# Regrouping TensorE's half-array products and postponing VectorE work in a fused mLSTM and Fourier-mixing kernel

## The chip, the cores and the metric

One core of one Trainium2 chip. The metric is the device time of one execution in microseconds; the profile's span is some 1.7 us shorter (421.29 and 419.6 for the kernel before). Every execution told of here was of the fast state. A ratio is the mean time of one kernel's fast runs over that of the kernel before in the same rounds, so it is not quite the ratio of the medians quoted beside it.

## The reference, cut to what matters

```python
# mLSTM cell: batch 4, 8 heads, 768 tokens, head size 40
for t in range(S):
    m_new = np.maximum(f_gate[:, :, t] + m, i_gate[:, :, t])
    ...
    C = f_stab * C + i_stab * np.einsum('bhd,bhe->bhde', vt, kt)
    n = f_stab * n + i_stab * kt
    y[:, :, t] = o * (C @ qt) / np.maximum(np.abs(n @ qt), 1.0)
# Fourier mixing, normalisation and an MLP of 320 -> 1280 -> 320
mixed = np.real(np.fft.fft(np.fft.fft(x, axis=1), axis=2))
u = x + mixed
un = (u - mu) / np.sqrt(var + 1e-06)
out = u + np.maximum(un @ w_ch1, 0.0) @ w_ch2
```

The kernel takes the recurrence in six chunks of 128 tokens per batch. While the MLP of batch b runs, the chunks of batch b+1 run beside it. Everything is placed by hand in slots, so that TensorE always has a product to do.

## The kernel before: the parts concerned

`at(slot, phase, ...)` enters work in a plan; the program is emitted in the order (slot, phase). The phases are EVAC 0, FILL 1, MAIN 2, FILL_PE 3. Engines run their own share of that order and wait for each other by semaphores.

```python
EVAC, FILL, MAIN, FILL_PE = range(4)
ps_s = pool("ps_s", 2, space=PSUM)
ps_h = pool("ps_h", 2, space=PSUM)     # ph, pc and (most) px take these two in turn
...
def mlstm_from_state(b, c):            # 128 rows: the full array (L479)
    k.ph = ps_h.tile([L, NP, L], FP, name="ph", tag="ph")
    ... nc.tensor.matmul(k.ph[:, p, :], k.C[:, p, :], k.qg[:, p, :], start=(p == 0), stop=False)
...
# in plan_mlstm(b, s0); chunk c is at s = s0 + 3 * c
at(s, FILL_PE + 2, mlstm_scores, b, c)              # 40 rows (L465)
at(s + 2, FILL, mlstm_weigh, b, c)                  # VectorE (L471)
at(s + 3, FILL_PE, mlstm_from_state, b, c)
at(s + 3, FILL_PE + 3, mlstm_from_chunk, b, c)      # L486
at(s + 3, FILL_PE + 3, mlstm_to_state, b, c)        # L496, into pc
t = s + (8, 8, 7, 5, 5, 5)[c]                       # batches after the first
at(t, FILL_PE + 1, mlstm_turn, b, c)                # transpose into px (L535)
at(t + 1, FILL + 0.05, mlstm_finish, b, c)          # VectorE reads px (L544 to L550)
...
def mlp_in(b, gr, f):                               # MLP of batch 0: 320 = 128 + 64 + 128 features
    if f % 2 == 0:
        k.pm = [bank("pm", [L, TG * L]) for _ in range(2)]
    for i, ch in ((1, 1),) if f % 2 else ((0, 0), (0, 1), (1, 0)):
        nc.tensor.matmul(k.pm[i], w1_sb[:, ch, f0:f0 + L], u[2 * ch], start=(ch == 0), stop=False)   # L837
    if f % 2:
        for i in range(2):                          # 64 rows each, side by side in the array (L841)
            r = slice(i * TAIL, (i + 1) * TAIL)
            nc.tensor.matmul(k.pm[i], w1t_sb[r, f // 2 * L:(f // 2 + 1) * L], u[1][r], start=False, stop=True)
...
# MLP of batches 1 to 3, one block in four slots (cut): L897 products, then the tails (L902, 64 rows)
add(h12, p5)                     # step 1, VectorE (L906): the first add
tails(1, (p3, p5)); tails(0, (p2, p1))
add(h12, p3); add(h22, p5); add(h11, p2)            # step 2: the other three
```

L479 and the like are lines of the kernel. A pair of 64-row products uses the two halves of the array at once: in the records the second starts 6 to 7 ns after the first. "Excursion" below means TensorE leaving the full array for such products and coming back. A PSUM bank holds what TensorE has summed until another engine has read it; only then can the next product that is given the bank start.

VectorE's other work has short names below. The finish of a chunk divides and writes its output. The conversions (L344 to L364, in part on ScalarE) prepare weights that have come in by DMA. The fold prepares the Fourier mixing's input, rstd is the reciprocal of the standard deviation (its steps alternate between VectorE and GpSimd), and the weight sum adds blocks of weights. GpSimd also makes each chunk's mask (L443) and scales its queries (L431).

## Time and profile before

| | before |
|---|---|
| median of the first 3 executions | 422.48 us (421.55 to 423.32) |
| span of the profile | 419.6 us |
| TensorE busy | 407.0 us, 97% |
| VectorE busy | 288.5 us, 69% |
| TensorE's idle gaps of over 30 ns, summed from the records | 9.5 us |

TensorE is the bound. Its idle time is small, so a reader should distrust the word "busy": the steps between its matmuls show where a busy TensorE runs slower than it can. The lines for this, and the waits, are in the prediction.

### The profile page before, as it was taken

The numbers are of one execution on the slowest core, as the hardware profiler recorded it, in microseconds if no ns is written. First come the engines' busy times: TensorE is split into PE (matmuls) and PEld (weight loads), VectorE is DVE, ScalarE is ACT, GpSimd is POOL, SyncE is SP. The second block draws the span as 40 slices with busy tenths as digits, with TensorE's granted clock in tenths as the row PEclk, the third lists the DMA queues.
The fourth block names the chain that finished last, engine by engine and source line by source line (L and its number), as shares of the span: only waits on it lengthen the run. The fifth ranks groups of instructions, "written<-read, shape, count | busy, mean of one in ns | idle before, by whom it ended". The sixth has DMA issues, their size and how long they took to land.

```text
span 419.6 us, 8013 instructions
## 1 busy us (share of the span) xinstructions
PE 407.0 (97%) x2966; PEld 304.0 (72%) x2966; DVE 288.5 (69%) x682; ACT 189.1 (45%) x493; POOL 112.9 (27%) x194
## 2 busy tenths in 40 slices
PE   8999999999999999999899999999999999999997
PEld 6877455566567778777458998977559988555996
DVE  8789895777995638795955578795854686335652
ACT  6986376586561222654356413654452023355000
POOL 5554201468331520342131440342120000020000
DMA  7899297557665144266200344310000000000010
GB/s 240 285 252 301 86 284 242 195 178 222 215 182 164 58 155 136 67 210 172 75 0 2 136 151 135 107 46 2 0 2 0 33 31 22 12 2 0 16 48 31
DMA packets 20549, 47.14 MB, mean 112 GB/s; under 512 B 2784, under 2 KB 9312, under 8 KB 20384
## 3 DMA queue, kind: packets, MB, share of 16 engines
q1 hardware_dynamic: 20512, 46.65, 35.8%
q8 instruction: 23, 0.38, 0.4%
q14 instruction: 14, 0.11, 0.1%
HBM read 42.52 MB, written 4.11 MB: 111 GB/s over the span
## 4 chain that ended last, share of the span: by engine, by line
PE 81%; DVE 12%; ACT 2%; issue 2%; DMA 1%; POOL 0%; DVEq 0%; ACTq 0%; POOLq 0%
PE po L1016 19%; PE pm L897 15%; PE po L960 8%; PE pm L837 5%; PE ps L465 5%; PE ph L486 5%; PE pm L902 4%; PE ph L479 4%; PE pu L729 4%; PE put L772 2%; PE px L535 2%; PE pz L698 2%; PE pm L841 1%; DMA raw<-in_w 1%; PE pz L686 1%
## 5 line engine op out<-in xcount | busy, mean ns | idle before, releaser
L966 DVE SCALAR_TENSOR_TENSOR x<-po,rstd,x 128x160 f32<-128x160 f32 (+1 forms) x69 | 27.0, 394 | 41.4 <-PE po L1016 35.5
L906 DVE TENSOR_TENSOR h<-h,pm 128x384 f32<-128x384 f32 x60 | 30.5, 549 | 31.4 <-PE pm L897 16.0
L421 ACT ACTIVATE W<-W,colT 128x128 f32<-128x128 f32 x144 | 45.0, 396 | 0.0
L443 POOL TENSOR_SCALAR_AFFINE_SELECT W<-W 128x1024 f32<-128x1024 f32 x18 | 21.3, 1183 | 79.8 <-ACT W L421 58.7
L897 PE MATMUL pm<-uT,w_sb 128*128 128x384 f32 x90 | 37.5, 503 | 1.8 <-DVE h L906 1.6
L960 PE MATMUL po<-w_sb,h 128*128 128x320 f32 x120 | 34.4, 435 | 0.0
L471 DVE TENSOR_TENSOR W<-ps,W 128x512 f32<-128x512 f32 x48 | 30.7, 680 | 4.5 <-POOL W L443 4.3
L837 PE MATMUL pm<-uT,w_sb 128*128 128x384 f32 x80 | 29.6, 499 | 0.7 <-DVE x L749 0.5
L777 ACT COPY uT<-put 128x384 f32<-128x384 f32 x24 | 11.2, 478 | 40.2 <-PE put L772 40.2
L960 PEld LDWEIGHTS po<-w_sb,h 128*128 128x128 f32 x120 | 22.2, 190 | 9.5 <-issue 0.8
L1016 PE MATMUL po<-T,S 128*128 128x160 f32 x180 | 27.9, 302 | 0.3 <-DVE x L966 0.3
L465 PE MATMUL ps<-qk 40*128 40x128 f32 x384 | 27.8, 284 | 0.0
L792 POOL TENSOR_TENSOR t<-rstd 128x6 f32<-128x6 f32 x12 | 3.1, 261 | 88.5 <-DVE v L790 87.9
L1016 PEld LDWEIGHTS po<-T,S 128*128 128x128 f32 x180 | 25.5, 190 | 1.7 <-DVE x L966 0.5
L897 PEld LDWEIGHTS pm<-uT,w_sb 128*128 128x128 f32 x90 | 15.5, 189 | 15.4 <-DVE h L906 7.7
L1016 PE MATMUL po<-w_sb,h 128*128 128x160 f32 x180 | 26.4, 301 | 0.0
L465 PEld LDWEIGHTS ps<-qk 40*128 40x128 f32 x384 | 23.4, 187 | 4.1 <-issue 0.7
L1016 PEld LDWEIGHTS po<-w_sb,h 128*128 128x128 f32 x180 | 25.1, 190 | 1.3 <-DVE x L966 0.3
L486 PE MATMUL ph<-W,kvt 128*41 128x128 f32 x384 | 25.8, 277 | 0.0
L524 ACT COPY h<-ph 41x512 f32<-41x512 f32 (+1 forms) x16 | 9.3, 583 | 36.2 <-PE ph L486 36.0
L431 POOL TENSOR_TENSOR qg<-qk,Gb 128x512 f32<-128x512 f32 x18 | 25.0, 1390 | 0.1
L479 PEld LDWEIGHTS ph<-qg,C 128*128 128x128 f32 x160 | 19.9, 191 | 6.8 <-issue 3.3
(207 smaller groups left out, 865.6 us busy)
## 6 DMA issues: line engine op xcount, KB each, us to landing
W<-M_d SPq DMA_DIRECT2D x18, 512.0 KB
kvt<-in_kv SPq DMA_DIRECT2D x24, 324.0 KB
qk<-in_qkT SPq DMA_DIRECT2D x48, 160.0 KB
raw<-in_w SPq DMA_DIRECT2D x10, 640.0 KB
Gb<-G_d SPq DMA_DIRECT2D x36, 128.0 KB
so<-in_o SPq DMA_DIRECT2D x24, 160.0 KB
out<-x SPq DMA_DIRECT2D x24, 160.0 KB
ds_sb<-in_dft_s SPq DMA_DIRECT2D x1, 1155.0 KB
```

Of the source, the lines that this page charges most:

```text
L421: nc.scalar.activation(out=k.W[:, h, :], in_=M, func=AF.Exp, scale=-1.0, bias=colT[:, c, 0, b * H + h:b * H + h + 1])
L431: nc.gpsimd.tensor_tensor(out=k.qg, in0=k.qk[:, 0], in1=k.Gb, op=OP.mult)
L465: nc.tensor.matmul(k.ps[hip][:, p, :], k.qk[r, 1, p, :], k.qk[r, 0, p, :], start=True, stop=True)
L471: nc.vector.tensor_tensor(out=Wv, in0=k.ps[hip], in1=Wv, op=OP.mult)
L479: nc.tensor.matmul(k.ph[:, p, :], k.C[:, p, :], k.qg[:, p, :], start=(p == 0), stop=False, skip_group_check=True)
L486: nc.tensor.matmul(k.ph[hip * 64:hip * 64 + D1, p, :], k.v1[:, 2 * p + hip, :], k.W[:, 2 * p + hip, :], start=(c == 0 and p == 0), stop=Tr ...
L837: nc.tensor.matmul(k.pm[i], w1_sb[:, ch, f0:f0 + L], u[2 * ch], start=(ch == 0), stop=False)
L897: nc.tensor.matmul(bank, w, u, start=start, stop=True, skip_group_check=True)
L906: nc.vector.tensor_tensor(out=h, in0=h, in1=bank, op=OP.add)
L960: nc.tensor.matmul(k.po, hidden(gr, f)[:, i * L:(i + 1) * L], w2_sb[:, f, :], start=(f == 0), stop=(f == NFF - 1))
L966: nc.vector.scalar_tensor_tensor(out=u, in0=po, scalar=k.rstd[:, c:c + 1], in1=u, op0=OP.mult, op1=OP.add)
L1016: nc.tensor.matmul(po, a[:, f], w[:, f], start=start and f == 0, stop=f == half - 1, skip_group_check=True)
```

## The change

Its intent is to make TensorE change between the full array and half-array products less often, and to take VectorE's less urgent work out of the way of the adds that free PSUM banks.

```diff
+    slots_of_halves = (32, 38, 50, 65, 97)
...
-            at(s + 2 if end else s + 3, FILL_PE, mlstm_from_state, b, c)
+            at(s + 2 if end else s + 3, MAIN - 0.1 if s + 3 in slots_of_halves else FILL_PE, mlstm_from_state, b, c)
...
-                t = s + (8, 8, 7, 5, 5, 5)[c]
+                t = s + (8, 8, 7, 7 if b == 1 else 5, 5, 5)[c]
...
-            at(x_done[j], FILL + 0.5 if b < 2 else FILL_PE + 0.2, mix_fold, b, p)
+            at(x_done[j] + (b > 1 and j == TG - 1), FILL + 0.5 if b < 2 else FILL_PE + 0.2, mix_fold, b, p)
...
+        ahead = gr == 1 and f // 2 in (1, 3)
         if f % 2 == 0:
-            k.pm = [bank("pm", [L, TG * L]) for _ in range(2)]
+            k.pm = k.pm_next if ahead else [bank("pm", [L, TG * L]) for _ in range(2)]
...
+        if f % 2 and not ahead:
+            between(k.pm, f // 2, False)           # the 64-feature products of this pair
+            if gr == 1 and f // 2 < NFF // 2 - 1:  # and those of the next pair, which start its banks
+                k.pm_next = [bank("pm", [L, TG * L]) for _ in range(2)]
+                between(k.pm_next, f // 2 + 1, True)
...
-        done = [s_mlstm + 3 * (j + NT // 2) + 7 for j in range(NT // 2)]
+        done = [s_mlstm + 3 * (j + NT // 2) + 7 + (b == 1 and j == 0) for j in range(NT // 2)]
...
-        at(s_mlp + NFF, FILL + 0.6, mix_rstd, b)
+        at(s_mlp + NFF + (2 if b > 0 else 0), FILL + 0.6, mix_rstd, b)
...
-        at((56, 57, 58, 72)[n], FILL + 0.4, out_weight_sums, n)
+        at((56, 57, 58, 75)[n], FILL + 0.4, out_weight_sums, n)
```

More of the change, by code (lines that the diff above doesn't have):

```diff
@@ L832, in mlp_in, with between @@
         u = [uT_bufs[gr][:, ch].rearrange("p c t -> p (c t)") for ch in range(3)]
+        def between(pm, n, start):
+            for i in range(2):
+                r = slice(i * TAIL, (i + 1) * TAIL)
+                nc.tensor.matmul(pm[i], w1t_sb[r, n * L:(n + 1) * L], u[1][r], start=start, stop=not start,
+                                 skip_group_check=True)
+        ahead = gr == 1 and f // 2 in (1, 3)
         if f % 2 == 0:
-            k.pm = [bank("pm", [L, TG * L]) for _ in range(2)]
+            k.pm = k.pm_next if ahead else [bank("pm", [L, TG * L]) for _ in range(2)]
         for i, ch in ((1, 1),) if f % 2 else ((0, 0), (0, 1), (1, 0)):
             f0 = (f // 2 * 2 + i) * L
-            nc.tensor.matmul(k.pm[i], w1_sb[:, ch, f0:f0 + L], u[2 * ch], start=(ch == 0), stop=False)
-        if f % 2:
-            for i in range(2):
-                r = slice(i * TAIL, (i + 1) * TAIL)
-                nc.tensor.matmul(k.pm[i], w1t_sb[r, f // 2 * L:(f // 2 + 1) * L], u[1][r], start=False, stop=True)
+            nc.tensor.matmul(k.pm[i], w1_sb[:, ch, f0:f0 + L], u[2 * ch], start=(ch == 0 and not ahead),
+                             stop=(ch == 1 and ahead), skip_group_check=True)
+        if f % 2 and not ahead:
[3 more added lines that the diff above has]
+                between(k.pm_next, f // 2 + 1, True)
     hid = {}
```

## The prediction

> **What bounds the kernel now.** I read the page's busy row first, then the chain that ended last, then who TensorE waited for, then the chain in order of time around each place that the diff touches.
>
> ```profile
> span 419.6 us, 8013 instructions
> PE 407.0 (97%) x2966; PEld 304.0 (72%) x2966; DVE 288.5 (69%) x682; ACT 189.1 (45%) x493; POOL 112.9 (27%) x194
> PE 81%; DVE 12%; ACT 2%; issue 2%; DMA 1%; POOL 0%; DVEq 0%; ACTq 0%; POOLq 0%
> PE pm L897 <- DVE h L906: 1.6, 2, 1.1
> PE ph L479 <- DVE den L544: 0.9, 1, 0.9
> ```
>
> TensorE is busy 97% and carries 81% of the chain, so only two things can shorten the program: less time inside TensorE's own stream, or fewer of its waits. The list of TensorE's waits is short. Summed over its gaps it idles about 9.5 us, and half of that lies before 60 us, where nothing changes. The last two lines above are the waits that the change can reach: 1.6 us in two stops of the MLP blocks (1.06 us at 207.94, 0.55 us at 301.97), and 0.9 us before one group of partial products from the state (L479) at 110.23.
>
> A busy TensorE hides a second cost. These are pieces of the chain in order of time (start, us until the next piece, what):
>
> ```profile
> 79.29 0.84 PE pm L841 x4
> 80.14 1.09 PE ph L479 x8
> 81.22 1.09 PE ps L465 x16
> ...
> 88.12 1.94 PE pm L837 x6
> 90.06 0.89 PE ph L479 x8
> 90.95 1.09 PE ps L465 x16
> ...
> 113.76 0.84 PE pm L837 x2
> 114.61 0.84 PE pm L841 x4
> 115.45 2.13 PE pm L837 x6
> ```
>
> L837 and L479 contract over 128 rows; L841 is the pair of 64-feature products, one on each half of the rows, and L465 works on 40 rows. After L837 the eight passes of L479 take 0.89 us; after L841 the same eight take 1.09. Six passes of L837 take 1.94 us in steady state and 2.13 after L841. So coming back to the full array costs 0.20 us. Going in costs as much: in the records the first L841 starts 416 ns after the last L837 where 322 is the steady step, and the next step is 420 where two products side by side repeat at 316. Going in and out is thus 0.20 + 0.20 = 0.40 us. From L841 straight into L465 (both on part of the rows) the records show no such step.
>
> **What the Trainium skill says.** The page "TensorEngine Tiling (Array Packing)", section "Key Properties", says that changing the tiling mode, and not merely the tile, drains TensorE, and that different tiles work in parallel. The trace agrees: about 0.1 us extra on each of two steps at every change of mode, and the second product of a pair starts 6 to 7 ns after the first. "SBUF — State Buffer", section "Who interferes with whom", says that only the port pair shared by VectorE and GpSimd contends, as an exclusive lock. The trace agrees where the weight conversion L358 takes 0.82 us at 91.28 and 1.64 at 111.64, beside GpSimd's mask (L443); this decides how soon VectorE is done below. "Perfetto Trace Analysis", section "Tensor Engine Instruction (MATMUL, LD_WEIGHTS)", says that TensorE's end times are computed, not observed; hence I use start-to-start steps.
>
> **The change, part by part.** The instructions are the same; ACT's and SP's order is unchanged, and only TensorE, VectorE and GpSimd are reordered.
>
> (1) The products from the state go ahead of the last MLP products of their slot. Of the five slots named, 32 holds none (batch 1 has 35, 38, ... 50), so four groups move: slots 38 and 50 in batch 1 (80.14 and 119.51 above), 65 in batch 2 (187.66) and 97 in batch 3 (282.49). Each stood between 64-row and 40-row products and so cost a way out and in again: 4 x 0.39 = 1.57 us gross.
>
> (2) The 64-feature products of two pairs stand together twice: two fewer excursions, 2 x 0.39 = 0.79 us gross. Starting a bank with them instead of with the 128-row product adds no instruction. The banks are free early enough: their ReLUs run at 88.67 and 99.13, and the banks are wanted after 94 and 105.
>
> (3) In batch 1 the turn of chunk 3 moves two slots back. Then L479 at 110.23 no longer needs the bank of the turn that VectorE finishes only at 110.09, and 0.91 us of wait goes. But the last L479 (slot 50) now needs the bank of this late turn. I follow VectorE: it ends the finish of chunk 2 near 109.7, then converts weights (2.5 to 3.5 us), adds the state (0.67), weighs (1.29) and finishes chunk 3 (1.65), which gives 116 to 117; TensorE arrives near 116.3. So nothing to 0.7 us comes back.
>
> (4) One place keeps TensorE from using what it gains: L479 of slot 44 waits for the query scaling on GpSimd (0.08 us now, at 99.18). GpSimd is full with 12 steps of rstd from 91.4 to 96.7, and only the 0.39 us of slot 38 moves it forward. TensorE would arrive about 0.8 us earlier and wait about 0.45.
>
> Sum for the first MLP (57.9 to 123): 4 x 0.39 (slots 38 and 50, and (2)) + 0.91 - 0.04 (an exit that was cheaper into the turn) - 0.4 - 0.3 = about 1.7 us.
>
> (5) Slots 65 and 97 gain a wait. The moved L479 (of batch 2 and 3, beside the MLP of the batch ahead) takes the bank of the turn of chunk 2, and in the built program it now waits for VectorE, which before it did not. In batch 2 VectorE ends that finish at 185.11 (L550 from 184.62 for 0.49 us), while TensorE would be there at 184.7: 0.5 us of wait against 0.39 saved, net -0.1. In batch 3 two subtractions are slowed by GpSimd (1.32 and 1.51 us instead of 0.56), so the finish ends at 280.42 and TensorE would be there at 279.2: L479 from 280.5, its 0.89, four L897 passes 1.29 and the tails 1.49 bring the scores to 284.2 instead of 283.58. Net -0.6. The 0.4 us that those tails now lose to a late add is already counted in 283.58.
>
> (6) Fold, rstd and weight sum move behind the MLP's adds. Here is why TensorE stands at 207.94, in the MLP of batch 1:
>
> ```profile
> 203.83 0.98 DVE L988 TENSOR_TENSOR w_sb<-w_sb 128x800 f32<-128x800 f32 x1
> 204.73 0.55 DVE L906 TENSOR_TENSOR h<-h,pm 128x384 f32<-128x384 f32 x1
> 207.34 1.48 DVE L906 TENSOR_TENSOR h<-h,pm 128x384 f32<-128x384 f32 x3
> 207.94 0.91 PE L897 MATMUL pm<-uT,w_sb 128*128 128x384 f32 x2 [1.06 <-DVE h L906]
> ```
>
> Between the first add and the other three VectorE does a fold and the start of rstd, from 205.19 to 207.34. In the new order the four adds come first. That frees 1.06 us, and 0.29 of the tails before it (1.85 us against 1.56), which waited for the first add behind the weight sum L988. The postponed work (fold 1.6, L638 0.5, L988 0.9, rstd 0.6: 3.6 to 4.1 us) must then fit before the next block's first add. The block repeats every 6.27 us, the adds end about 2.35 after the tails begin, and the add takes 0.55: 3.4 us are free. It runs over by 0.2 to 0.6: net 1.35 - 0.4 = +0.95. In the MLP of batch 2 (301.97) there is no L988, the postponed work is 2.8 us and fits, and the whole 0.55 is gained. In the last MLP rstd held up nothing.
>
> Total: 1.7 - 0.1 - 0.6 + 0.95 + 0.55 = 2.5 us. From the median 422.48 this is 420.0.
>
> **The rivals.** (a) All of the gross gain stays: 6 x 0.39 + 0.91 + 1.35 + 0.55 = 5.2 us, 417.3. For it: those 97%. Against it: the waits for VectorE that appear in the built program at slots 50, 65 and 97. (b) The waits are worse than I count: the late finish of chunk 3 meets weight conversions slowed by GpSimd (1.64 to 1.89 us each in this stretch instead of 0.82), slot 50 stands for 2 us, and with the over-run in (6) nothing is left: 422 to 422.5. (c) The DMA decides the first MLP: the chain there holds 5.77 us of a weight transfer, from 100.34 to 106.16, ahead of VectorE's work. If it lands when it did, and not 0.4 us earlier, 0.4 of the 1.7 go. Against it: its issue follows GpSimd's scaling, which itself moves forward.
>
> **Range and chances.** The three executions before spread 421.55 to 423.32, so a median carries some 0.7 us of its own; my terms (3) to (6) are each good to half a microsecond or so. That gives 418.2 to 421.7. Faster by over 2% would need 8.4 us, beyond even rival (a); slower by over 2% needs a long new stall that no listed wait suggests. I put 0.02, 0.97 and 0.01.
>
> **What would show it.** In the chain or the records: eight passes of L479 at 0.89 us in slots 38, 65 and 97; eight passes of L841 together (about 1.47 us) twice; no wait of L897 on L906 in the MLP of batch 2 (before at 301.97), and one of at most 0.6 us in that of batch 1; no wait at the old 110.23; new waits of L479 on VectorE near 185 (0.5 us) and 280 (1.3 us), and on GpSimd near 99 (0.45 us). I am wrong if L479's first step after L837 is not at its steady value, if the bank waits of slots 65 and 97 do not show, or if the postponed fold makes tails stand longer than 0.6 us.

## The result, and the profile after

The changed kernel took 419.86 us (median of 4, 419.79 to 420.98) beside 422.86 us for the kernel before, ratio 0.994 (95% interval 0.9911 to 0.9969). Sixteen further runs, in the last set of experiments, gave 420.11 us and 0.9954 (0.9935 to 0.9973). Of some 422 us the two ratios are 2.5 and 1.9 us.

The program grew by 15 lines, so the same work has other line numbers after: L837 is L850, L897 is L912, the tails L902 are L917, the adds L906 are L921, the weight sum L988 is L1003. L465, L479, L486, L535 and L841 keep theirs. First the page of the changed kernel:

```profile
span 418.1 us, 8020 instructions
...
PE 405.1 (97%) x2966; PEld 304.0 (73%) x2966; DVE 287.8 (69%) x682; ACT 188.9 (45%) x493; POOL 115.3 (28%) x194
```

And its list of TensorE's waits (us in total, times, longest):

```profile
PE ph L479 <- DVE x L550: 1.8, 3, 1.3
...
PE ph L479 <- POOL qg L431: 0.3, 1, 0.3
```

The waits of L897 for L906 (1.6 us) and of L479 for L544 (0.9 us) are gone. In their place L479 waits three times for L550, the last instruction of a finish, 1.8 us in all, and once for GpSimd. The busy share is unchanged, which shows again that it says little here.

Now TensorE in order of time (start, length, engine, line and operation; in brackets the idle time before it and who ended it). The length of a row includes the computed end of its last matmul; the time that it takes in the stream is the difference of two starts.

```profile
79.41 1.05 PE L479 MATMUL ph<-qg,C 128*128 128x128 f32 x8
80.30 0.81 PE L850 MATMUL pm<-uT,w_sb 128*128 128x384 f32 x2
...
94.66 1.56 PE L841 MATMUL pm<-uT,w1t_sb 64*128 64x384 f32 x8
96.15 2.20 PE L850 MATMUL pm<-uT,w_sb 128*128 128x384 f32 x6
...
98.62 0.81 PE L850 MATMUL pm<-uT,w_sb 128*128 128x384 f32 x2
99.74 1.16 PE L479 MATMUL ph<-qg,C 128*128 128x128 f32 x8 [0.30 <-POOL qg L431]
...
183.36 0.60 PE L535 MATMUL px<-ident,h 128*128 128x128 f32 x4
184.34 1.13 PE L479 MATMUL ph<-qg,C 128*128 128x128 f32 x8 [0.38 <-DVE x L550]
...
277.10 0.60 PE L535 MATMUL px<-ident,h 128*128 128x128 f32 x4
278.96 1.13 PE L479 MATMUL ph<-qg,C 128*128 128x128 f32 x8 [1.26 <-DVE x L550]
279.93 0.81 PE L912 MATMUL pm<-uT,raw 128*128 128x384 f32 x2
```

In slot 38 the eight passes of L479 take 80.30 - 79.41 = 0.89 us, where they took 1.09 before. The eight passes of two pairs together take 96.15 - 94.66 = 1.49 us for one excursion. The third to fifth parts show the new waits: for GpSimd at 99.74, and for the banks that VectorE had yet to read at 184.34 and 278.96. In slot 47, where the kernel before waited at 110.23, L479 now starts at 109.98, while VectorE ends the finish of chunk 2 only at 110.38: with the later turn it no longer needs that bank.

Then the MLP of batch 1, where the kernel before stood at 207.94, VectorE and TensorE in one list:

```profile
205.29 1.48 DVE L921 TENSOR_TENSOR h<-h,pm 128x384 f32<-128x384 f32 x3 [1.50 <-PE pm L917]
...
205.90 0.91 PE L912 MATMUL pm<-uT,w_sb 128*128 128x384 f32 x2
...
208.94 0.98 DVE L1003 TENSOR_TENSOR w_sb<-w_sb 128x800 f32<-128x800 f32 x1
...
210.52 0.54 DVE L921 TENSOR_TENSOR h<-h,pm 128x384 f32<-128x384 f32 x1
...
210.61 2.06 PE L917 MATMUL pm<-uT,w1t_sb 64*128 64x384 f32 x8
...
212.60 0.91 PE L912 MATMUL pm<-uT,w_sb 128*128 128x384 f32 x2
```

L912 no longer stands at 205.90. But the first add of the next block begins only at 210.52, behind the postponed fold, sum and rstd, and the tails that need it take 212.60 - 210.61 = 1.99 us, where those of the block before take 1.56 (from 204.34 to 205.90).

To set the parts of the prediction against the records, I cut the program at starts of L486 (the products of a chunk with its own tokens) that both traces have:

| stretch | before | after | difference | predicted |
|---|---|---|---|---|
| MLP of batch 0: batch 1 chunk 0 to batch 2 chunk 0 | 72.05 to 132.43: 60.38 | 72.99 to 131.51: 58.52 | -1.86 | -1.7 |
| slot 65: batch 2 chunk 3 to 4 | 179.84 to 189.77: 9.93 | 178.93 to 189.08: 10.15 | +0.22 | +0.1 |
| MLP of batch 1: batch 2 chunk 5 to batch 3 chunk 0 | 195.83 to 234.48: 38.65 | 195.14 to 232.89: 37.75 | -0.90 | -0.95 |
| slot 97: batch 3 chunk 3 to 4 | 274.27 to 284.60: 10.33 | 272.66 to 283.70: 11.04 | +0.71 | +0.6 |
| MLP of batch 2 to the end: from batch 3 chunk 5 | 290.66 to 419.55: 128.89 | 289.76 to 418.10: 128.34 | -0.55 | -0.55 |
| sum | | | -2.38 | -2.5 |

The spans differ by 1.5 us only, because the stretch up to 72 us was 0.94 longer in this profile. No instruction there has moved. VectorE's step L344 waits for a weight transfer; the first line is of the kernel before, the second of the changed one:

```profile
67.12 0.49 DVE L344 TENSOR_SCALAR e<-raw 128x640 uint32<-128x640 uint32 x1 [4.42 <-DMA raw<-in_w]
```

```profile
68.64 0.49 DVE L344 TENSOR_SCALAR e<-raw 128x640 uint32<-128x640 uint32 x1 [6.17 <-DMA raw<-in_w]
...
71.05 0.91 PE L850 MATMUL pm<-uT,w_sb 128*128 128x384 f32 x2 [0.90 <-DMA qk<-in_qkT]
```

The last of these lines is the stop of TensorE that follows in the changed kernel. The profile puts it down to another transfer. But ScalarE works on after L344 before it empties the bank that L850 needs, and in all eleven profiles with such a stop the product after it starts 2.41 or 2.42 us after L344, whatever releaser is named. So I read the weight transfer as the cause.

Over all thirteen profiles of this study the first L486 of batch 1 starts anywhere from 72.05 to 74.24 us, with the same instructions ahead of it. A part of the spread between executions sits there. The table above leaves it out, and so do the readings below. Each reading of a stretch is of one execution. From slot 65 on, the stretches that no edit touched agree within 0.03 us in all profiles. In the first MLP the three other profiles with the changed kernel's order, at full clock and without a late transfer, took 58.63 to 58.65 us where the table has 58.52.

### The profile page after: what moved, and what is told of

The parts are those of the page before. It is cut to its first block, busy times and chain, and to the rows that moved or that the text cites. A ratio compares the mean times of both kernels' runs of the same rounds, so it can differ in the third digit from the quotient of the medians.

```text
span 418.1 us, 8020 instructions
## 1 busy us (share of the span) xinstructions
PE 405.1 (97%) x2966; PEld 304.0 (73%) x2966; DVE 287.8 (69%) x682; ACT 188.9 (45%) x493; POOL 115.3 (28%) x194
## 4 chain that ended last, share of the span: by engine, by line
PE 75%; DVE 14%; DMA 5%; ACT 2%; issue 2%; POOL 0%; DVEq 0%; ACTq 0%; POOLq 0%; SPq 0%
PE po L1031 18%; PE pm L912 16%; PE po L975 8%; PE pm L917 5%; PE ps L465 4%; PE ph L486 4%; DMA kvt<-in_kv 4%; PE ph L479 3%; PE pu L733 3%; PE pm L850 2%; DVE W L471 2%; PE px L535 2%; DMA qk<-in_qkT 2%; PE pz L702 2%; PE put L776 1%
## 5 line engine op out<-in xcount | busy, mean ns | idle before, releaser
L921 DVE TENSOR_TENSOR h<-h,pm 128x384 f32<-128x384 f32 x60 | 30.6, 549 | 32.5 <-PE pm L917 19.4
L443 POOL TENSOR_SCALAR_AFFINE_SELECT W<-W 128x1024 f32<-128x1024 f32 x18 | 21.9, 1218 | 80.6 <-ACT W L421 56.3
L912 PE MATMUL pm<-uT,w_sb 128*128 128x384 f32 x90 | 37.5, 503 | 0.2 <-DVE uT L900 0.2
L850 PE MATMUL pm<-uT,w_sb 128*128 128x384 f32 x80 | 30.0, 500 | 1.6 <-DMA qk<-in_qkT 0.9
L465 PE MATMUL ps<-qk 40*128 40x128 f32 x384 | 27.4, 282 | 0.0
L465 PEld LDWEIGHTS ps<-qk 40*128 40x128 f32 x384 | 23.7, 187 | 4.7 <-issue 0.7
L486 PE MATMUL ph<-W,kvt 128*41 128x128 f32 x384 | 25.8, 277 | 0.0
L912 PEld LDWEIGHTS pm<-uT,w_sb 128*128 128x128 f32 x90 | 15.5, 189 | 13.7 <-DVE h L921 6.0
L479 PEld LDWEIGHTS ph<-qg,C 128*128 128x128 f32 x160 | 20.0, 191 | 6.3 <-issue 2.6
L479 PE MATMUL ph<-qg,C 128*128 128x128 f32 x160 | 21.6, 278 | 2.9 <-DVE x L550 1.8
```

Source lines behind the costliest of these rows:

```text
L465: nc.tensor.matmul(k.ps[hip][:, p, :], k.qk[r, 1, p, :], k.qk[r, 0, p, :], start=True, stop=True)
L486: nc.tensor.matmul(k.ph[hip * 64:hip * 64 + D1, p, :], k.v1[:, 2 * p + hip, :], k.W[:, 2 * p + hip, :], start=(c == 0 and p == 0), stop=Tr ...
L912: nc.tensor.matmul(bank, w, u, start=start, stop=True, skip_group_check=True)
L921: nc.vector.tensor_tensor(out=h, in0=h, in1=bank, op=OP.add)
```

## The experiments

Each kernel was correct and ran in five rounds. The first eight ran on one chip: four in one set with 37 runs of the kernel before (422.15 us), four in a second set with 26 (422.12). The last three ran on another chip with 21 (422.36). Kernels of different sets are compared by their ratios to the kernel before.

**The moves alone.** Fold, rstd and weight sum as in the change, in the kernel before.

```diff
+ x_done[j] + (b > 1 and j == TG - 1)        # fold
+ s_mlp + NFF + (2 if b > 0 else 0)          # rstd
+ (56, 57, 58, 75)[n]                        # weight sum
```

> The kernel before with only the fold, rstd and weight-sum moves (part 6). My theory: VectorE's adds come first, so the waits of the MLP products on the adds go: in the MLP of batch 1 about 0.9 us net (1.35 us freed, at most 0.6 of it lost again in the tails), in the MLP of batch 2 about 0.55 us; the first MLP is unchanged (the wait of 0.9 us near 110 stays). Time 421.0 to 421.4 against 422.5 to 422.9 of before, ratio 0.9965. Rival (the reordering inside TensorE is what pays, these moves pay nothing since VectorE's work is only postponed): ratio 1.000 and a wait of a microsecond one block later.

420.85 us, ratio 0.9968 (0.9957 to 0.9979). From batch 2 chunk 3 to batch 3 chunk 0 it took 53.73 us against 54.64 before (-0.91), the end 128.36 against 128.89 (-0.53), and no L897 waited for an add. The rival falls: postponing VectorE's work is worth more than half of the whole gain.

**TensorE's part alone.** The changed kernel with these three lines put back.

```diff
- x_done[j] + (b > 1 and j == TG - 1)
- s_mlp + NFF + (2 if b > 0 else 0)
- (56, 57, 58, 75)[n]
```

> The changed kernel with fold, rstd and weight sum put back (parts 1, 2, 3 alone). My theory: the first MLP gains some 1.7 us, slots 65 and 97 lose about 0.2 and 0.7 us, the MLP blocks of batch 1 and 2 keep their waits for the adds of about 1.06 and 0.55 us. Time about 421.5, ratio 0.998. If all the mode changes saved came through (6 times 0.39 us and the 0.9 us wait) the ratio would be 0.992.

421.41 us, ratio 0.9983 (0.9973 to 0.9993). The first stretch took 58.64 us (-1.74), and at 184.78 and 280.32 L479 waited 0.38 and 1.27 us as in the changed kernel. The product of this ratio and the last is 0.9951, the changed kernel's own 0.9954: within the intervals the two parts simply add.

**Only slots 38 and 50.**

```diff
-    slots_of_halves = (32, 38, 50, 65, 97)
+    slots_of_halves = (38, 50)
```

> The changed kernel with only slots 38 and 50 in the list, so the products of slots 65 and 97 stand again behind the MLP's tails. My theory: the bank of the late turn is what these two wait for, so undoing them gives back about 0.2 us at slot 65 and 0.7 us at slot 97: ratio to before 0.992, about 0.9 us under the changed kernel, with no wait of L479 near 184 and 279. Rival (a mode change saved is always a gain, the wait would stand elsewhere anyway): 0.8 us slower than the changed kernel, ratio 0.996.

419.24 us, ratio 0.9925 (0.9906 to 0.9943). From batch 2 chunk 3 to batch 3 chunk 0 it took 53.74 us instead of 53.96, and the piece of slot 97 is back at its 10.33. Both new waits are gone. So the moves of slots 65 and 97 cost 0.22 and 0.71 us net, though each saves an excursion; the rival, that a saved change of mode always pays, falls. (Slot 32, left out here too, holds no such products.)

**The late turn in every batch.** If the bank is the cause, another bank must cure it.

```diff
-                t = s + (8, 8, 7, 7 if b == 1 else 5, 5, 5)[c]
+                t = s + (8, 8, 7, 7, 5, 5)[c]
...
-        ... + 7 + (b == 1 and j == 0) for j ...
+        ... + 7 + (b > 0 and j == 0) for j ...
```

> The changed kernel with the turn of chunk 3 two slots later in batches 2 and 3 too, as the change has it in batch 1, with the fold that needs it one slot later. The moved products of slots 65 and 97 then take the bank of a state sum that VectorE has long read. My theory: no wait for VectorE at these two, each saves its 0.39 us, so slot 65 gains 0.6 and slot 97 gains 1.1 us over the changed kernel: ratio to before about 0.990. Rival: the later finish of chunk 3 pushes VectorE's adds back and the products of the next blocks wait for them by as much, or the last products from the state wait for the bank of the late turn: ratio 0.994 or more, with new waits of L912 on L921 or of L479 a slot or three later.

418.13 us, ratio 0.9901 (0.9881 to 0.9922). TensorE in this kernel, at slots 65 and 97:

```profile
182.33 0.81 PE L912 MATMUL pm<-raw 128*128 128x384 f32 x2
182.97 1.05 PE L479 MATMUL ph<-qg,C 128*128 128x128 f32 x8
183.86 0.81 PE L912 MATMUL pm<-uT,raw 128*128 128x384 f32 x2
...
276.09 1.05 PE L479 MATMUL ph<-qg,C 128*128 128x128 f32 x8
```

And the end of VectorE's finish of chunk 2 at slot 65:

```profile
183.31 0.49 DVE L550 TENSOR_TENSOR x<-px,so 128x320 f32<-128x320 f32 x1
```

L479 starts without a wait and takes 0.89 us. The stretch from batch 2 chunk 3 to batch 3 chunk 0 fell from 53.96 to 53.34 us, that from batch 3 chunk 3 to chunk 5 from 17.10 to 15.60. That is 0.62 and 1.50 us. L479 no longer waits for the finish at all: VectorE ended it at 183.80, 0.83 us after L479 had started, and at slot 97 at 277.81, 1.72 us after. So the bank, not the products or VectorE's load, was the cause.

The 1.50 us are more than the 1.1 that I expected, which was 0.71 + 0.39. The rest is the late add that the prediction mentions. In the kernel before, VectorE came to the first add of this block behind a finish and ended it at 280.88, when the tails had begun:

```profile
280.53 1.96 PE L902 MATMUL pm<-uT,w1t_sb 64*128 64x384 f32 x8
```

From their start to that of L479 it took 1.89 us instead of 1.49. In the changed kernel the add is done before the tails begin, so these 0.40 us were gone and hid a part of the new wait: 1.50 - 0.39 - 0.40 = 0.71.

**Rstd of batch 0 three slots later.** The query scaling on GpSimd, for which L479 waits at 99.74, comes behind the 12 steps of rstd.

```diff
-        at(s_mlp + NFF + (2 if b > 0 else 0), FILL + 0.6, mix_rstd, b)
+        at(s_mlp + NFF + (2 if b > 0 else 3), FILL + 0.6, mix_rstd, b)
```

> The changed kernel with the rstd of batch 0 three slots later, so that its 12 steps on GpSimd no longer stand ahead of the mask and the query scaling of chunk 3. My theory: the wait of L479 for GpSimd near 99 (0.30 us in the changed kernel's profile) goes and nothing takes its place: about 0.3 us under the changed kernel, ratio to before about 0.9938, if the changed kernel is at 0.9946. Rival: GpSimd only does the same work later and the mask of chunk 4 comes late, or the weight transfer sets the pace of this stretch: no gain, and L479 near 110 or the weighing before it waits for GpSimd.

420.41 us, ratio 0.997 (0.9956 to 0.9984). The expected gain did not come; that it is slower than the changed kernel (0.9954) is inside the intervals, and only the trace shows it. This miss is the most telling one. The wait did go, and the piece from chunk 2 to 3 of batch 1 (L486 to L486) took 8.84 us instead of 9.41. But further on GpSimd, VectorE and TensorE show:

```profile
106.09 1.09 POOL L443 TENSOR_SCALAR_AFFINE_SELECT W<-W 128x1024 f32<-128x1024 f32 x1
...
107.22 1.29 DVE L471 TENSOR_TENSOR W<-ps,W 128x512 f32<-128x512 f32 x2 [2.60 <-POOL W L443]
...
117.90 1.13 PE L479 MATMUL ph<-qg,C 128*128 128x128 f32 x8 [1.69 <-DVE x L550]
```

The mask of chunk 4 (L443) now stands behind rstd, so VectorE stands 2.60 us before it can weigh. Its next conversions L358 and L360 then overlap the mask and the query scaling of chunk 5 on GpSimd and take 1.43 and 1.90 us where the changed kernel's profile has 0.81 and 0.82; only L364 after them is shorter there (0.82 instead of 1.59). Its finish of chunk 3 ends at 117.75, 0.64 us later than in the changed kernel, while TensorE wants the bank 0.9 us earlier. The piece from chunk 4 to 5 took 10.17 us instead of 8.65. A gain of 0.57 turned into a net loss of 0.95, in the very wait that the prediction's rival (b) feared.

**Without the pairs.**

```diff
-        ahead = gr == 1 and f // 2 in (1, 3)
+        ahead = False
...
-            if gr == 1 and f // 2 < NFF // 2 - 1:
+            if False:
```

> The changed kernel with part 2 undone: every pair's 64-feature products behind its own 128-row products. My theory: two excursions of 0.39 us come back, 0.79 us, of which 0.3 us is hidden, because L479 of slot 44 then reaches its wait for GpSimd later and does not stand: net 0.5 us slower than the changed kernel, ratio to before 0.9957. If the wait for GpSimd stays or the turn of slot 50 catches up, 0.8 us or 0.3 us. Rival (the products starting a bank cost or save something of their own): a difference outside 0.2 to 0.9 us, or other step times than 316, 416 and 420 ns in the pairs.

419.50 us, ratio 0.9933 (0.9913 to 0.9953), which cannot be told from the changed kernel's. The trace can tell them: the first stretch took 58.82 us, 0.29 more. Around the first pair (chunk 2 to 3 of batch 1) it was 0.08 shorter, around the second (chunk 3 to 5, 19.16 us against 18.78, which four other profiles have within 0.01) 0.38 longer. The second pair is worth its whole excursion and the first nothing, since TensorE only comes to GpSimd's wait earlier:

```profile
98.53 0.92 PE L841 MATMUL pm<-uT,w1t_sb 64*128 64x384 f32 x4
99.46 1.16 PE L479 MATMUL ph<-qg,C 128*128 128x128 f32 x8
```

Without the pair L479 starts 0.93 us after L841, 0.08 more than an excursion makes it, in place of the wait at 99.74. The expected 0.5 us was too much.

**The early turn.** Part 3 undone.

```diff
-                t = s + (8, 8, 7, 7 if b == 1 else 5, 5, 5)[c]
+                t = s + (8, 8, 7, 5, 5, 5)[c]
...
-        ... + 7 + (b == 1 and j == 0) for j ...
+        ... + 7 for j ...
```

> The changed kernel with part 3 undone: the turn of chunk 3 of batch 1 where it was before. My theory: L479 of slot 47 again takes the bank that VectorE has yet to read and stands some 0.9 us near 110, more by the 0.3 us or so that TensorE comes there earlier now; the 0.17 us wait of slot 50 goes: 0.6 to 1.0 us slower than the changed kernel, ratio to before 0.9965. Rival (the bank was never the cause, the weight transfer ahead of VectorE's work was): the same time as the changed kernel, since that transfer lands when it does.

420.61 us, ratio 0.9955 (0.9939 to 0.9970): by whole runs no difference to the changed kernel, as the rival had it; only the trace speaks against the rival. There L479 near 112 waits for VectorE again (0.52 us idle) and that of slot 50 no longer does; from chunk 3 to 5 it took 19.30 us instead of 18.78. So the turn's move is worth 0.52 us net in this kernel, a little less than expected. That the transfer is not the cause shows in the kernel with the moves alone, which has the early turn too: VectorE stood for no transfer between 104 and 112, and L479 at 111.13 still stood 0.64 us. The transfer may add to the size: in the kernel before VectorE stood 0.47 us for it, and L479 0.91.

What is left, a first stretch longer by another 0.45, is a piece (chunk 2 to 3: 9.86 us) that was as long in the late-turn kernel and not in others. In these two profiles another weight transfer came late; this is the late-turn kernel:

```profile
96.50 1.09 DVE L344 TENSOR_SCALAR e<-raw 128x640 uint32<-128x640 uint32 x1 [2.52 <-DMA raw<-in_w]
```

VectorE stood 2.52 and 2.40 us for it, and 0.89 in the changed kernel; its weighing, and the scores (L465) that need the banks it reads, came late. I do not count these 0.45 us for or against either kernel.

**Late turn, late rstd and a later weight sum.**

```diff
 (late turn as above)
+        at(s_mlp + NFF + (2 if b > 0 else 3), FILL + 0.6, mix_rstd, b)
+        at((56, 57, 58, 77)[n], FILL + 0.4, out_weight_sums, n)
```

> The kernel with the late turn in all batches, and on top of it the rstd of batch 0 three slots later and the last weight sum two slots later, between the first add of a block and the other three. My theory: the tails of the third block in the MLP of batch 1, which took 2.0 us instead of 1.49 because the first add came behind the weight sum, fall to 1.49 (0.5 us), and the wait for GpSimd near 99 goes (0.2 to 0.3 us). Against the late-turn kernel 0.7 us less: ratio to before 0.9885, about 417.4 us. Rival: the weight sum then holds up the three later adds and the products of the next block wait for them instead: no more than 0.2 us gained.

419.07 us, ratio 0.9920 (0.9900 to 0.9940), where 0.9885 was expected. The tails did fall (the next product starts 1.55 us after them), but L479 of slot 50 stood 1.88 us for VectorE, for the reason just found. It was sent together with the kernel that showed it. The three that follow were made after it.

**Late turn and later weight sum.** Rstd left alone.

> The late-turn kernel with the last weight sum between the first add of a block and the other three, and nothing done to the rstd of batch 0. My theory: the tails of the third block in the MLP of batch 1 fall from 2.0 us to 1.49, so 0.5 us less than the late-turn kernel: ratio to before 0.989. Rival: as with the late rstd, something further on takes it back: 0.990 or more.

416.65 us, ratio 0.9862 (0.9837 to 0.9888). From batch 2 chunk 3 to batch 3 chunk 0: 52.89 us against 53.34 of the late-turn kernel. These 0.45 us are a little under the 0.5 expected: the tails fell to 1.56 us (210.81 to 212.37), not to 1.49. The ratio fell by more than that (0.4% of the time is 1.6 us). The traces do not show the rest, but the two were timed in different sets and on different chips, and the width of the two intervals allows for it: 0.45 us is 0.11%, and each interval reaches 0.2% or more to either side.

**The changed kernel again**, in the same rounds.

> The changed kernel once more, in the same runs as the two others. From the sums of the parts (moves alone 0.9968, TensorE's part alone 0.9983) its ratio should be 0.9951, from the two-slot kernel's 0.9925 and the 0.9 us that the two slots cost 0.9946; measured so far 0.994 in four runs. I expect 0.9935 to 0.9955; near 99 a wait for GpSimd of 0.2 to 0.5 us, at slot 65 a wait for VectorE of 0.38 and at slot 97 of 1.26 us again.

420.11 us, ratio 0.9954 (0.9935 to 0.9973), with idle times of 0.41, 0.37, 0.38 and 1.27 us before L479 at 103.11, 120.82, 187.89 and 282.51. Its profile caught a slower execution (span 421.6, mean granted clock 0.97 between 58 and 124 us), so I read no stretch of the first MLP from it.

**Rstd behind everything.** Late turn, later weight sum, and rstd of batch 0 eight slots later, when GpSimd has done its masks.

```diff
+        at(s_mlp + NFF + (2 if b > 0 else 8), FILL + 0.6, mix_rstd, b)
```

> The kernel of the first of these three with the rstd of batch 0 eight slots later, behind the fold, when GpSimd has done the masks and query scalings of chunks 3 to 5. My theory: what spoilt the first attempt was that rstd then stood ahead of the mask of chunk 4, so VectorE weighed late and its finish of chunk 3 came 1.7 us after TensorE wanted the bank. Behind them it holds up nobody: the first MLP's stretch from slot 44 to the end of slot 50 gains 0.5 to 0.7 us, L479 of slot 50 waits under 0.3 us. Ratio to before 0.9875. Rival: the pace of VectorE there is set by its own conversions and the mask of chunk 5 beside them, so L479 of slot 50 stands 1 us or more again and nothing is gained.

416.47 us, ratio 0.9852 (0.9826 to 0.9877), the best of all and faster than both kernels. TensorE at slot 44, and its list of waits:

```profile
98.60 0.81 PE L850 MATMUL pm<-uT,w_sb 128*128 128x384 f32 x2
99.24 0.94 PE L479 MATMUL ph<-qg,C 128*128 128x128 f32 x7
```

```profile
PE ph L479 <- DVE x L550: 0.2, 1, 0.2
```

The wait for GpSimd is gone, that of slot 50 is 0.18 us, and the first stretch took 57.96 us, 0.69 less than without the move of rstd. By whole runs these last two kernels cannot be told apart; the trace puts the second ahead.

## Why the prediction was right

The forecast was 420.0 us in 418.2 to 421.7; 419.86 came, and 420.11 in the larger set. It was right by its steps, as the table of stretches shows: each stretch came within 0.2 us. Inside the first MLP there was some luck: three waits were priced too low, and their errors nearly cancel, as told below.

- **The cost of an excursion, 0.40 us.** It held. L479 behind the full array takes 0.89 us in slot 38, and pairs together cost one excursion. The piece with slot 38 (chunk 0 to 1 of batch 1) fell from 10.20 to 9.79 us, and undoing the second pair cost 0.38. The moves of slots 38 and 50 were not undone by themselves; their gain rests on these steps.
- **Term (3), the turn's bank.** The wait near 110 went, and a smaller one came to slot 50, 0.17 us idle, within the "nothing to 0.7" (0.42 by the steps). Rival (b) described what happens when VectorE is later still; the late rstd made it happen.
- **Term (4), GpSimd's wait at slot 44.** I expected about 0.45 us; the changed kernel's profile has 0.30, and the kernels with the same order there 0.17 to 0.43. What I did not say is that it makes the first pair worthless.
- **Term (5), new bank waits at slots 65 and 97.** Forecast 0.5 and 1.3 us, idle 0.38 and 1.26; net +0.22 and +0.71 against +0.1 and +0.6. Changing the bank removed both, so the cause is shown.
- **Term (6), the moves.** -0.95 and -0.55 forecast, -0.90 and -0.55 measured, and the same in the kernel with the moves alone. The over-run of 0.2 to 0.6 was 0.43 us of tails, and moving the weight sum took it away. (By the prediction's own figures, 3.6 to 4.1 less 3.4, it would be 0.2 to 0.7.)
- **The other rivals.** (a), that all of the gross gain of 5.2 us stays, falls with the waits just named. (c), that the DMA decides the first MLP, did not hold in the changed kernel's profile, where L344 at 106.33 did not wait for the transfer; but another one came late in two of the other profiles and cost 0.45 us there.

Slightly off was my price of a wait. I took the idle column, 0.91 us at 110.23, for the loss. The steps say more. At 278.96 L479 should have started 0.44 us after L535 (the length of that piece in the chains before), at 277.54. It started 1.42 us later than that, and its passes took 0.97 us instead of 0.89: 1.50 lost where the column shows 1.26. At 184.34 the same sum gives 0.54 + 0.08 = 0.62 for a column of 0.38. By the same account the wait removed at 110.23 was worth 1.14, the 0.17 of slot 50 costs 0.42, and the 0.30 of slot 44 some 0.6. These errors have opposite signs and nearly cancel: 4 x 0.39 + 1.14 - 0.42 - 0.6 + 0.16 (a stop at slot 44 that was there before, of 0.08 idle) - 0.04 is 1.8 us for the first MLP, and 1.86 was measured.

What stays open is the pace of the weight transfers before 72 us: the start of batch 1 lies up to 2.2 us apart between the profiles.

## What to carry to other kernels

On a saturated TensorE, count how often products of different array modes follow one another, and put a full-array product beside its like; but before moving a product earlier, ask which PSUM bank it takes and when the last reader of that bank is done. Work that is not urgent goes behind what frees a bank, also on the engine that is far from being the bound: more than half of this gain (1.45 of 2.38 us in the table) was VectorE's order alone. When a wait is removed, look for the next user of the same engine; the late rstd removed one wait of 0.3 us and made one of 1.7.

## What the Trainium skill lacked or had wrong

- "TensorEngine Tiling (Array Packing)", "Key Properties", says that a change of tiling mode drains TensorE but gives no price. Here leaving the full array and coming back costs 0.40 us, in four steps of about 0.1 us (416 and 420 ns instead of 322 and 316 going in, 413 and 213 instead of 316 and 112 coming back). It also does not say in which mode 40-row products run; here going from 64-row pairs straight to them costs nothing extra (a step of 316 ns).
- "Perfetto Trace Analysis", "Tensor Engine Instruction (MATMUL, LD_WEIGHTS)", says that TensorE's end times are computed, but not what follows for its idle time: three stops before L479, each behind L535, cost 0.24 or 0.25 us more than the idle column shows (1.26 shown, 1.50 lost; 0.38 and 0.62; 0.17 and 0.42), and a fourth some 0.3 more (0.30 shown, 0.6 lost).
- No page that I used says whether an accumulation begun by two half-array products costs time; here the two steps of a pair that begins a bank are 316 ns each, the steady step between pairs of this kind. The steps of going in, 416 and 420 ns, were seen only on pairs that end a bank.
